# Attention with part of its exponentials on VectorE: one of three bit shifts becomes an accumulating DMA

## The chip, the core and the metric

The kernel runs on one core of a Trainium2 chip. The core has TensorE (PE), VectorE (DVE), ScalarE (ACT), GpSimd (POOL) and SyncE (SP), each with an instruction queue of its own that it works through in order, and 16 DMA engines that serve the queues of SP, ACT and POOL. The metric is the time of one execution on the device in microseconds (us), as a median of several runs. The profile shows one further execution, in which every instruction is recorded.

## The reference

Two attention blocks over the same 2048 tokens of width 512 with 32 heads of 16, mixed by a gate:

```python
def _A_ref(x, wqkv, wo):                       # B, S, D, H = 1, 2048, 512, 32
    q, k, v = ...                              # x @ wqkv, split into heads
    scores = jnp.einsum("bhqd,bhkd->bhqk", q, k) * (Dh ** -0.5)
    p = _softmax(scores, axis=-1)
    o = jnp.einsum("bhqk,bhkd->bhqd", p, v)
    return (...)(o) @ wo

def _B_ref(x, wqkv, w_phi, wo):                # linear attention
    phi_q = concat([softmax(q @ w_phi), softmax(-(q @ w_phi))])
    phi_k = ...                                # the same of k
    kv, z = ...                                # sums of phi_k * v and of phi_k over the tokens
    o = (phi_q @ kv) / (phi_q @ z + 1e-6)
    return (...)(o) @ wo

g = _sigmoid((x * gate_w).sum(-1, keepdims=True))
return g * a + (1 - g) * b
```

Nearly all the time goes to branch A: 32 heads x 2048 x 2048 scores, an exponential of each, and their product with the values. All inputs are bfloat16.

## The kernel before

Branch A is cut into 512 *packs*. A pack is one block of 128 keys (`kt`, 16 of them) for one chunk of 512 queries (`qc`, 4 of them) and 4 heads (`g8`, 8 groups): four score tiles of 128 keys x 512 queries. The 16 packs of one `(qc, g8)` are a *group*; there are 32. For each tile PE makes the scores into PSUM (`_scores`, L963, four tiles side by side in the array), an engine makes the exponentials, and PE adds exponentials times values into one accumulator bank (`_values`, L1077, again four tiles side by side). The denominators come from a column of ones among the values. `_norm` then transposes, divides and transposes back, on VectorE and, for all but the last groups, by way of 16 small `turned` copies and a DMA transpose on SP's queue.

The exponentials are made in two ways:

- By ACT, most of them: `_exp`, L1011, takes three tiles and two tiles in turn from a ring of five PSUM banks and writes `ET`. The score group after next (`_qk`) may start only when ACT has freed the banks.
- By VectorE, for the packs in `spot` (listed by `AWAY`, a bit mask for each group, at the places `KT0 + KTS * n`): `_vector_bits`, L903, multiplies the scores by a constant, adds another, and writes the result as unsigned 16-bit integers in `va`. Read as bfloat16 these bits are a straight-line approximation of the exponential. `_vector_terms`, L919, makes three copies of the bits shifted by 30, 62 and 95 in `vp`, for two packs at once. `_pv_terms` adds four products into the accumulator: `va` and the first copy with the values `V`, the second and third copy with `vc`, the values times 0.75 (`o_vc`). The sum of the four lines is a closer approximation.

Beside this, PE, VectorE and SP carry the projections of q, k and v (`_proj*`, with 8 small DMAs that place each query tile in `qT`, L677), the gate (`_gate`), and branch B (`_b_*`), spread over the whole span. PE also runs matmuls on zeros (`_fill`, L1084) and on unused data (`pads`, L984).

The order on every engine is not that of the program text. `Plan.order` sets up all operations with assumed lengths (`cost`), latencies (`lat`) and due times (`prio`), moves the due times by the hand-written-out list `SHIFT`, and lists the operations engine by engine: whatever can start first goes first, ties by due time. `Plan.emit` writes these five queues out, with semaphore waits where an operation needs another engine's. So any changed length moves operations everywhere, and in the chip an operation that is late holds up all that stands behind it in its engine's queue.

At the end, the last group's normalization (`_norm_last`) runs in two halves of 256 columns, and the last four output tiles (`_out`) are evicted by VectorE (two) and ACT (two).

## Time and profile before

| | |
|---|---|
| median of 3 runs | 759.11 us (758.89 to 759.82) |
| the profiled execution | 759.64 us, of which the span from the first to the last instruction is 757.8 us |
| mean granted TensorE clock | 0.999 of full speed |
| 20 us stretches from 40 to 740 us: ACT busy | 19.39 us or more in each |
| the same stretches: VectorE busy | 16.55 us (40 to 60), 18.51 to 20.00 in the others |
| DMA queue of SP: share of the 16 engines' span | 13.8%, 20.10 MB |
| last exponential ends | 748.63 us |

An engine's busy time is the time in which at least one of its instructions ran; consecutive instructions overlap a little, so that the mean of one is longer than its share of the busy time. "Idle before" is time in which the engine stood still just before an instruction of the group, and the name behind the arrow is what ended most of it. The timeline gives the start, the length, the engine, the line of the code and the shapes, with equal neighbours merged.

### The profile page before, as it was taken

How to read it: one execution, taken by the hardware profiler on the slowest of the kernel's cores; microseconds unless marked ns; L12 is line 12 of the kernel's file. 1: busy time of each engine (PE TensorE's matmuls, PEld its weight loads, DVE VectorE, ACT ScalarE, POOL GpSimd, SP SyncE). 2: the span in 40 equal slices, each digit the busy share in tenths (PEclk: the TensorE clock that was granted, in tenths of full speed). 3: DMA queues.
4: the chain of work that ended last, by engine and by line, in shares of the span. 5: the costliest groups of instructions: out<-in, count | busy, mean ns of one | idle time of the engine just before them, and what ended most of it. 6: DMA issues, size and time to landing. Idle time of an engine off the chain costs nothing.

```text
span 757.8 us, 16775 instructions
## 1 busy us (share of the span) xinstructions
PE 718.0 (95%) x7172; PEld 229.8 (30%) x7241; DVE 730.0 (96%) x1138; ACT 740.4 (98%) x646; POOL 8.1 (1%) x17
## 2 busy tenths in 40 slices
PE   8999999999999999999999999999999998999997
PEld 3334333342322232232222222223232222222222
DVE  6989899999999999999999999999999999999997
ACT  6999999999999999999999999999999999999995
POOL 3000000000000000000000000000000000000000
PEclk9999999999999999999999999999999999999999
DMA  9300100000010010000003101411103102301120
GB/s 212 130 2 1 15 8 10 14 7 16 2 16 8 8 16 8 6 11 7 18 9 63 23 12 25 71 29 23 29 29 65 21 16 35 78 13 25 12 26 29
DMA packets 88745, 21.68 MB, mean 29 GB/s; under 512 B 81632, under 2 KB 88160, under 8 KB 88672
## 3 DMA queue, kind: packets, MB, share of 16 engines
q1 hardware_dynamic: 86944, 20.10, 13.8%
q8 instruction: 56, 0.92, 0.5%
q10 hardware_dynamic: 1728, 0.52, 0.3%
q14 instruction: 17, 0.14, 0.1%
HBM read 4.21 MB, written 2.10 MB: 8 GB/s over the span
## 4 chain that ended last, share of the span: by engine, by line
ACT 64%; DVE 21%; PE 12%; DMA 1%; issue 1%; SPq 1%; DVEq 0%
ACT ET L1011 62%; DVE va L903 9%; DVE vp L919 6%; PE ps L963 5%; PE ps L1077 3%; ACT bq L1281 3%; PE ps L641 2%; DVE btree L1270 1%; DVE bq L1279 1%; PE ps L714 1%; DVE T L1129 1%; SPq L677 1%; DMA xT<-in_A_x_dram 1%; PE ps L984 1%; DVE V L720 1%
## 5 line engine op out<-in xcount | busy, mean ns | idle before, releaser
L1011 ACT ACTIVATE ET<-ps 128x1536 bf16<-128x1536 f32 x626 | 712.2, 1345 | 7.1 <-PE ps L963 6.2
L963 PE MATMUL ps<-qT,kT 32*128 32x512 bf16 x2048 | 312.1, 384 | 17.7 <-ACT ET L1011 8.5
L903 DVE TENSOR_SCALAR va<-ps 128x512 uint16<-128x512 f32 x484 | 314.4, 681 | 6.3 <-PE ps L963 4.9
L919 DVE TENSOR_SCALAR vp<-va 128x4096 uint16<-128x4096 uint16 (+1 forms) x204 | 221.6, 1097 | 0.2
L963 PEld LDWEIGHTS ps<-qT,kT 32*128 32x128 bf16 x2048 | 80.8, 91 | 263.0 <-ACT ET L1011 157.2
L1077 PE MATMUL ps<-ET,V 128*32 128x512 bf16 x1564 | 149.0, 386 | 0.3
L1077 PE MATMUL ps<-vp,vc 128*32 128x512 bf16 x968 | 84.5, 384 | 0.9 <-DVE vp L919 0.9
L1077 PEld LDWEIGHTS ps<-ET,V 128*32 128x32 bf16 x1564 | 39.3, 95 | 65.0 <-issue 51.0
L641 PE MATMUL ps<-WB,xT 128*128 128x512 bf16 x169 | 50.8, 383 | 4.4 <-issue 1.5
L1084 PE MATMUL ps<-kT,zero 128*32 128x512 bf16 x580 | 50.2, 385 | 0.0
L1077 PE MATMUL ps<-va,V 128*32 128x512 bf16 x484 | 47.8, 385 | 0.0
L1077 PE MATMUL ps<-vp,V 128*32 128x512 bf16 x484 | 46.2, 384 | 0.7 <-DVE vp L919 0.6
L641 PE MATMUL ps<-xT,WA 128*128 128x512 bf16 (+1 forms) x107 | 30.6, 373 | 3.6 <-issue 2.3
L1077 PEld LDWEIGHTS ps<-vp,vc 128*32 128x32 bf16 x968 | 21.9, 95 | 35.2 <-issue 18.0
L1281 ACT ACTIVATE bq<-bq 128x2048 bf16<-128x2048 bf16 x16 | 32.1, 2024 | 0.0
L1252 DVE CAST bq<-ps 128x512 bf16<-128x512 f32 x32 | 21.7, 683 | 2.9 <-PE ps L641 2.8
L1129 DVE STREAM_TRANSPOSE T<-ps 128x512 f32<-128x512 f32 x31 | 22.0, 709 | 0.6 <-PE ps L1077 0.3
L714 PE MATMUL ps<-WA,xT 128*128 128x128 bf16 x256 | 20.4, 220 | 0.5 <-DVE V L720 0.3
L1457 PE MATMUL ps<-WoA,onTA 128*128 128x512 bf16 x62 | 19.3, 382 | 1.0 <-DVE onTA L1117 0.9
L1279 DVE TENSOR_TENSOR bq<-bq,btree 128x2048 bf16<-128x2048 bf16 x16 | 19.4, 1214 | 0.0
L1084 PEld LDWEIGHTS ps<-kT,zero 128*32 128x32 bf16 x580 | 12.6, 94 | 22.1 <-issue 20.3
L641 PEld LDWEIGHTS ps<-WB,xT 128*128 128x128 bf16 x192 | 11.9, 97 | 23.9 <-issue 14.4
(87 smaller groups left out, 346.2 us busy)
## 6 DMA issues: line engine op xcount, KB each, us to landing
turned<-T SPq DMA_DIRECT2D x240, 8.0 KB, 1.8
qT<-qs SPq DMA_DIRECT2D x120, 16.0 KB, 1.8
WB<-in_B_wqkv_dram SPq DMA_DIRECT2D x1, 1536.0 KB, 7.4
out_dram<-WB SPq DMA_DIRECT2D x12, 128.0 KB, 1.9
WA<-in_A_wqkv_dram SPq DMA_DIRECT2D x3, 384.0 KB, 5.6
WoA<-in_A_wo_dram SPq DMA_DIRECT2D x1, 512.0 KB, 8.5
WoB<-in_B_wo_dram SPq DMA_DIRECT2D x1, 512.0 KB, 8.3
WA<-in_A_wqkv_dram ACTq DMA_DIRECT2D x3, 128.0 KB, 4.0
```

The lines of the kernel that those rows point to most:

```text
L641: ins = e.matmul(self._bank(job)[:, 0:n], lhs(c), rhs(c), start=(c == 0), stop=(c == 3))
L714: ins = e.matmul(self._bank(job)[:, P * tt:P * tt + P], self.xT[:, c, QCH * j + TOK * tt:QCH * j + TOK * tt + TOK], self.WA[:, 2, c, P * c ...
L903: parts.append(op("DVE", lambda e, j=j, job=job: e.tensor_scalar(self.va[:, pair, side, j, :], self._bank(job), SCALE * LOG2E * 128.0, (12 ...
L919: self.plan.op("DVE", lambda e, k=k, shift=shift: e.tensor_scalar(flat(self.vp[:, k]), flat(self.va[:, pair]), float(shift), None, op0=ALU ...
L963: return e.matmul(out, self.kT[32 * i:32 * i + 32, cp, kt * TOK:(kt + 1) * TOK], self.qT[32 * i:32 * i + 32, s, :], start=True, stop=True, ...
L1011: o = plan.op("ACT", lambda e: e.activation(self.ET[:, a % NS:a % NS + n, :], self.ps[:, self._ring(a):self._ring(a) + n, :], ACT.Exp, sca ...
L1077: ins = e.matmul(self._bank(ot)[32 * i:32 * i + 32, :], V[:, v0:v0 + 32], tile(), start=(kt == 0), stop=(kt == self.NT - 1), tile_position ...
L1084: ins = e.matmul(self._bank(ot)[32 * i:32 * i + 32, :], self.zero[:], self.kT[:, 0, 0:QCH], start=False, stop=False, tile_position=(0, 32 ...
L1129: op("DVE", lambda e: e.transpose(T1[:, side].rearrange("p b s -> p (b s)"), src()), 0.635, deps=last, writes=[b_T1[side]], name="n_t1", p ...
L1252: [lambda e, b, k=k: e.tensor_copy(bq[:, k].rearrange("p (g s v) -> p g s v", g=8, s=2)[:, :, 0, :], b.rearrange("p (g v) -> p g v", g=8))],
L1279: run("b_sub", two(2048), lambda e, out=out, t=t: e.tensor_tensor(out, p, spread(t[:, :, 0], 32), ALU.subtract), at, [pos, tree[side]], [buf])
L1281: op("ACT", lambda e, side=side: e.activation(sides[side], sides[side], ACT.Exp, scale=1.0 - 2 * side), self.c_act(2048) + 0.04, reads=[bu ...
```

## The change

- The first of the three shifts is no longer a copy. The first value product reads `va` as it is; then 30 is added to `va` in place; then the second value product reads `va` again. The two other shifts stay copies.
- The addition in place is a DMA on POOL's queue for 116 packs (`accum_op=ALU.add`, from `step`, a tensor in DRAM of 128 x 2048 numbers 30, written once at the start by a DMA from `va`, which POOL has filled), and an operation of VectorE for the ten packs in `IN_PLACE` (those of the last two groups). Each place of `va` has a semaphore of its own that counts its additions.
- `va` has three pairs of places in place of two, `vp` two shifts in place of three.
- The packs that VectorE works on stand at every second place (1, 3, 5, 7, 9 of a group) and no longer at every third, and are 126 in place of 121.
- The gate's sums are computed by narrow matmuls (32 columns of output rows, four chunks of queries side by side) into one bank, with one transpose, and spread by 16 small DMAs on SP's queue.
- The last group is normalized as the others before it, without halves; the order of the last output products changes.
- Assumed latencies of the query copies, `turned` copies and DMA transposes become longer, the due times and the whole list `SHIFT` are new, so that the order on every engine is another.

```diff
-SHIFTS = ((30, 0), (62, 1), (95, 1))
+SHIFTS = ((62, 1), (95, 1))
+FIRST_SHIFT = 30
...
-                if o.name.startswith("dma"):
+                if o.slot is not None:
+
+                    if o.slot not in places:
+                        places[o.slot] = ctx.enter_context(nc.semaphore(f"place{o.slot}"))
+                    count[o.slot] = count.get(o.slot, 0) + 16
+                    o.sem = (places[o.slot], count[o.slot])
+                elif o.name.startswith("dma"):
...
-    NB, LEAD = 4, 16.0
+    NB, LEAD, NVA = 4, 12.0, 3
+    VALUES, IN_PLACE, SLACK = 6.0, (480, 481, 482, 483, 484, 485, 486, 487, 488, 489, 490, 491, 492, 493, 494, 495, 496, 497, 498, 499, 500, 501, 502, 503, 504, 505, 506, 507, 508, 509, 510, 511), 6.0
...
-    KT0, KTS, NKT = 1, 3, 5
-    KEEP = 13
+    KT0, KTS, NKT = 1, 2, 5
+    KEEP = 14
...
-    TURN = 1.5
-    LAST, RAMP, PART = 8.0, 48, 24
-    STEP, BITS, TERM, PVX, NORM, QDUE, PUT = 0.625, -80, 5.5, 0.8, 2, -22.0, 3.8
+    TURN = 3.2
+    ADD, LANDING = 3.1, 2.6
+    LAST, RAMP, PART = 6.0, 48, 24
+    STEP, BITS, TERM, PVX, NORM, QDUE, PUT = 0.5, -40, -4, 0.8, 2, -22.0, 3.8
...
+        row = self.va[:, 0, 0].rearrange("p n q -> p (n q)")
+        o = op("POOL", lambda e: e.memset(row, FIRST_SHIFT), 2.0, prio=-60)
+        self.o_step = self.dma("SP", "step", lambda e: e.dma_start(self.step, row), cost=0.6, deps=[o], prio=-8, lat=4.0)
...
-                 prio=due, lat=1.6)
+                 prio=due, lat=2.8)
...
-            m = op("PE", mm, 4 * self.c_pe(512), reads=[self.b_xT[qc], b_gwb], name="gate", prio=self.GATE + qc, rel=self.GATE - 6,
-                   acquire=job)
...
+        def mm(e):
+            for c in range(4):
+                for qc in range(NQC):
+                    ins = e.matmul(self._bank(job)[32 * qc:32 * qc + 32, :], self.gwb[:, c, :],
+                                   self.xT[:, c, QCH * qc:QCH * qc + QCH], start=(c == 0), stop=(c == 3),
+                                   tile_position=(0, 32 * qc), skip_group_check=True)
+            return ins
...
+        parts = [lambda e, qc=qc, h=h: e.dma_start(self.gh[32 * h:32 * h + 32, :, qc, :], g[32 * qc:32 * qc + 32])
+                 for qc in range(NQC) for h in range(4)]
+        d = self.dma("SP", "gate", parts, cost=0.6 * len(parts), writes=[self.b_g], deps=[a], prio=self.GATE + 5, lat=1.6)
...
+        self.by_dma = self.spot - set(self.IN_PLACE)
...
+        pair, side = self.slots.pop(p)
+        va, b_va = self.va[:, pair, side], self.b_va[pair][side]
+        group = 16 * g
+
+        def values(tile, deps, reads, prio, tag, V=None):
+            src = {i: lambda i=i: tile()[:, i, :].bitcast(BF16) for i in range(4)}
+            x = self.plan.op("PE", lambda e: self._values(e, ot, g8, kt, src, V), 0.23, deps=deps, reads=reads, name="pvx",
+                             prio=prio, kind="col", array=0.2133)
+            x.tiles, x.tag = [0, 1, 2, 3], tag
+            self.late.append(x)
+            return x
+        ready = [self.pvs[self.NT * g]] + self.b_V[g8 // 2][kt // 4].writers
+
+        first = values(lambda: va, ready, [b_va], max(group + 1, p - self.VALUES), f"i{p}")
+        if p in self.by_dma:
+            add = self.dma("POOL", f"add{p}", lambda e: e.dma_start(va.rearrange("p n q -> p (n q)"), self.step, accum_op=ALU.add),
+                           cost=self.ADD, deps=b_va.readers + [self.o_step], prio=p - self.VALUES + 1, lat=self.LANDING)
+            add.slot = 2 * pair + side
+            add.fn = [add.fn]
+        else:
+            flat = va.rearrange("p n q -> p (n q)")
+            add = self.plan.op("DVE", lambda e: e.tensor_scalar(flat, flat, float(FIRST_SHIFT), None, op0=ALU.add),
+                               0.07 + self.NB * QCH * 0.00026, deps=list(b_va.readers), name="v_step", prio=p - self.VALUES + 1)
+        add.tag = f"i{p}"
+        b_va.readers = [values(lambda: va, ready + [add], [], p + self.PVX, f"x{p}")]
...
-        if g == self.NPACK // self.NT - 1:
-            return self._norm_last(qc, lambda: self._bank(self.ot[g]), last, self.onTA[:, qc % 2, g8 // 2, :], 16 * g + 17.0,
-                                   self.ot[g])
...
-                     lat=1.6)
+                     lat=2.6)
...
-                b_on = self.b_last[tt // 2] if final and pr == 3 else b_onTA[pr]
-                m = op("PE", mm, self.c_pe(512), reads=[b_on, self.b_WoA], deps=[m], name="outa",
-                       prio=due + (final and pr == 3), acquire=job if alone else None)
+                m = op("PE", mm, self.c_pe(512), reads=[b_onTA[pr], self.b_WoA], deps=[m], name="outa",
+                       prio=self.NPACK + 5 + (1, 0, 3, 2)[tt] if final and pr == 3 else due, acquire=job if alone else None)
```

In `_values` nothing changes; `_vector_terms` now hands `_pv_terms` the place of `va` (`self.slots`) and only the two remaining copies.

## The prediction

> **What bounds the kernel now.** I read the page's totals first, then the groups of instructions with shapes kept apart, then the table of waits, the DMA issues, and the timeline of the end.
>
> ```profile
> span 757.8 us, 16775 instructions
> PE 718.0 (95%) x7172; PEld 229.8 (30%) x7241; DVE 730.0 (96%) x1138; ACT 740.4 (98%) x646; POOL 8.1 (1%) x17
> ...
> L1011 ACT ACTIVATE ET<-ps 128x1536 bf16<-128x1536 f32 x626 | 712.2, 1345 | 7.1 <-PE ps L963 6.2
> L903 DVE TENSOR_SCALAR va<-ps 128x512 uint16<-128x512 f32 x484 | 314.4, 681 | 6.3 <-PE ps L963 4.9
> ```
>
> ScalarE (ACT) sets the time: 740.4 of 757.8 us busy, 712.2 of them exponentials. They cover 313 x 3 + 312 x 2 + 1 = 1564 score tiles, so a tile costs 712.2 / 1564 = 0.455 us, and an average exponential 712.2 / 626 = 1.14 us. Their idle is 7.1 us, of which 4.9 is one wait before the first. VectorE, at 96%, is nearly a second bound; POOL has nothing to do. So the time can fall only by taking tiles from ACT, and only if PE keeps it fed.
>
> ```profile
> PEld ps L963 <- ACT ET L1011: 157.2, 396, 1.0
> ...
> ACT ET L1011 <- PE ps L963: 6.2, 5, 4.9
> ```
>
> The first line is PE's cover: 396 times a score group stood ready and waited for ACT, 157.2 / 396 = 0.40 us each. A hold-up of PE's queue shorter than that costs nothing; what is longer reaches ACT. The second shows that it now hardly ever does.
>
> **The change, part by part.** The counts come from the two programs' order of instructions.
>
> *ACT.* 121 VectorE packs become 126: exponentials 313 + 312 + 1 become 309 + 308 + 1, that is 20 tiles fewer, 20 x 0.455 = -9.1 us on the path that sets the end. The gate's exponential shrinks from 128x128 to 128x32, -0.1 us.
>
> *VectorE.*
>
> ```profile
> L919 DVE TENSOR_SCALAR vp<-va 128x4096 uint16<-128x4096 uint16 x159 | 191.5, 1214 | 0.2
> ...
> L919 DVE TENSOR_SCALAR vp<-va 128x2048 uint16<-128x2048 uint16 x45 | 30.1, 682 | 0.0
> ```
>
> The bits grow from 484 to 504: +20 x 0.650 = +13.0. The shifts fall from 159 wide and 45 narrow to 116 and 20: 116 x 1.204 + 20 x 0.669 = 153.1 against 221.6, -68.5. Ten in-place adds of the narrow shape: +6.7. Three gate transposes fewer at 0.71: -2.1; the unsplit last norm -0.9. So 730 becomes 678 us, 91% of a span near 748. It is off the path, the gain is only room.
>
> *PE.* Values 3500 to 3560 matmuls, fillers 580 to 660, pads 56 to 34, gate 16 full ones to 16 narrow ones. At 0.095, 0.087 and 0.34 us of busy time each (149.0 / 1564, 50.2 / 580, 15.4 / 45): +5.7 + 7.0 - 7.5, and about -2.7 for the gate. The total stays within 3 us of 718; the 0.40 us waits hide it. Without them it would cost those 3 us.
>
> *SyncE.* Sixteen gate copies follow the first query load. Sixteen `turned` copies took 11.21 us to issue (74.16 in the timeline), so about 11 us; the queue was empty from 34 to 74 us, which hides them, and the first norm's `turned` waits behind them. The `step` store sits between WB (issued at 16.20) and WoA, which moves two weight loads that nobody needs before branch B's output by some 0.5 us. If that room were gone the first query load would be late instead, and it stands ahead of them.
>
> *The end.*
>
> ```profile
> 749.79 0.45 DVE L1107 STREAM_TRANSPOSE T<-ps 128x256 f32<-128x256 f32 x1 [0.55 <-PE ps L1077]
> ...
> 752.90 0.60 ACT L1468 ACTIVATE xT<-ps 128x512 bf16<-128x512 f32 x1 [4.27 <-PE ps L1457]
> ...
> 753.24 0.45 DVE L1117 STREAM_TRANSPOSE onTA<-T 128x256 bf16<-128x256 bf16 x1
> ...
> 754.38 0.60 ACT L1468 ACTIVATE xT<-ps 128x512 bf16<-128x512 f32 x1 [0.89 <-PE ps L1457]
> ```
>
> Now the last norm runs in two halves, from 749.79 to the last eviction's end at 754.98: 5.2 us. Unsplit: transpose 0.71, product 0.17, reciprocal 0.20, multiply 0.42, transpose 0.71, with gaps 2.3; first output matmul 0.39 and its delay 0.1; two evictions of 0.69 in a row on VectorE (ACT's two run beside them): 4.2 us. So -1.0.
>
> *The adds.* POOL issues 116 accumulating DMAs of 128x2048 uint16, 512 KB each, and PE waits for each before it reads `va` the second time. Behind that wait on PE stand the next score group and so the next exponential. Behind an add on POOL stands the next add only. No row of before has such a DMA. Nearest rows:
>
> ```profile
> WB<-in_B_wqkv_dram SPq DMA_DIRECT2D x1, 1536.0 KB, 7.4
> out_dram<-WB SPq DMA_DIRECT2D x12, 128.0 KB, 1.9
> WoA<-in_A_wo_dram SPq DMA_DIRECT2D x1, 512.0 KB, 8.5
> ```
>
> Between 128 KB (1.9 us) and 1536 KB (7.4 us) lie 3.9 us per 1000 KB, so 512 KB lands after 3.4 us if it is alone, and 1024 KB, since an add also reads its destination, after 5.4. WoA's 8.5 was queued with two other loads. The issue itself: 0.43 us is the single one of WB on SP's queue; the order in the diff assumes ADD = 3.1 on POOL and then LANDING = 2.6. Low end 0.43 + 3.4 = 3.8 us from release to landing, high end 3.1 + 5.4 = 8.5. I take the diff's sum, 5.7: it lies between the two, near their middle of 6.2, and the change calls its lengths recorded.
>
> What the order allows I counted as exponentials between the point where an add is released (first read on PE, and VectorE's shifts of that tile) and the PE group that needs it: 4 for five adds, 5 for three, 6 for 24, 7 for 16, 8 or more for 68. At 1.14 us that is 4.55, 5.7, 6.8, 8.0 and more. At 5.7 only the five are late, by 1.15 us, of which 0.40 is covered: 5 x 0.75 = +3.8 us. At 3.8 nothing is late. At 8.5, 48 are: 5 x 3.95 + 3 x 2.8 + 24 x 1.7 + 16 x 0.5 - 48 x 0.40 = +58 us. For the second of a pair POOL has two issues to do: 2 x 3.1 + 2.6 = 8.8, and those have 9 or more exponentials, 10.3 us.
>
> The Trainium skill (DMA: Bandwidth & Descriptors, "Anatomy of one DMA — SWDGE (gpsimd) path") fits a DMA issued from POOL at 2.0 us plus its bytes at 436 GB/s; an estimate from that page is 3.2 us for 512 KB and 4.4 for twice that, so by it no add is late and the sum is 3.8 us lower. The rows of before can't test it, as POOL issued nothing.
>
> *The sum.* 757.8 - 9.1 - 0.1 - 1.0 + 3.8 = 751.4 us of span. Around the span lay 759.64 - 757.8 = 1.8 us, and the profiled execution stood 0.5 above the median 759.11. So 751.4 + 1.8 - 0.5 = 752.7, rounded to 752.5.
>
> **The rivals.**
>
> *A, late adds hold PE (slower).* If release to landing is over the order's 5.7 us, each of the tight adds stops PE's queue with the score groups behind it. The gain of 10.2 us is eaten from 6.7 us on: 5 x (2.15 - 0.40) + 3 x (1.0 - 0.40) = 10.6. At 7.5: 5 x 2.95 + 3 x 1.8 + 24 x 0.7 - 32 x 0.40 = 24, so 747.6 + 24 + 1.3 = 773 us; at 8.0 it is +40 and 789. For it: the high end 8.5 is above 6.7, and the adds share the DMA engines with `turned` and query copies, which the diff now plans at 2.6 and 2.8 us where the trace has 1.8. Against it: the engines are 15% busy, and two thirds of the adds are far from tight.
>
> *B, POOL's issuing and VectorE's shifts get in each other's way.* The price: if a shift could not run while POOL issues, 116 x 3.1 = 360 us, 48% of the span, would be closed to 146 shifts and in-place adds, each waiting 1.55 us on average when it meets one: 146 x 0.48 x 1.55 = 109 us, VectorE 787, and with its idle 28 us 815. It decides from some 42 us on (748 - 678 - 28). With issues of 0.43 us it would cost 146 x 0.07 x 0.2 = 2 us and show nowhere. In before both engines work at once only in the first 21 us, too short to tell. The Trainium skill (SBUF — State Buffer, "SBUF: two separate sides") has such a rule: VectorE in a two-port mode and GpSimd take turns at a shared port pair, and descriptors issued from GpSimd wait meanwhile. By that rule the adds get longer too, by up to one shift, and A is likelier; no run here shows it yet.
>
> *C, no change.* PE, at 95% busy, takes back the 10 us in switches between scores and values of five more packs. Against it stands the 157.2 us of waiting for ACT. 758 to 760 us.
>
> **How the numbers follow.** 0.2% of 759, 1.5 us, is about what a measurement tells from no change. Forecast 0.50, with its own range 746 (nothing late, ACT's small gaps gone as well) to 757; A 0.36; B 0.07; C 0.07. Faster 0.50, all of it the forecast; slower 0.42, A and B less a hundredth that falls within; same 0.08. The range runs from 746 to 788, A up to a total of 8.0 us; left out are B, A's upper part and a little below.
>
> **What would show it.** Right: 618 exponentials at 1.14 us, ACT idle of some 12 us, VectorE near 91%, hardly any wait of the value matmuls on `va` for a DMA, and adds landing within 6 us of their release. Wrong: waits of PE for `va`'s DMA by the dozen with ACT's idle for scores grown by tens of us (A); shifts longer than 1.2 us or gaps before them, VectorE still at 96% or more (B); the exponentials fewer, but gaps before them ended by scores that waited for nothing but PE's own work (C). An eviction end more than 4.7 us after the last norm's start would make the end's term wrong.

## The result and the profile after

| | before | changed |
|---|---|---|
| median | 759.24 us (758.89 to 759.82) | 817.84 us (811.18 to 827.13) |
| the profiled execution's span | 757.8 us | 812.9 us |
| mean granted TensorE clock | 0.999 | 0.953 |

The ratio is 1.0742, with a 95% interval of 1.066 to 1.0824: the change makes the kernel 7% slower. 752.5 us was forecast. Of the four runs after, the one at 827.13 us was in a slower state; the other three have a median of 814.66, and from here on differences and the table below use such undisturbed runs alone.

The totals of the page after:

```profile
span 812.9 us, 17167 instructions
PE 747.4 (92%) x7359; PEld 228.6 (28%) x7359; DVE 692.6 (85%) x1092; ACT 738.2 (91%) x638; POOL 117.2 (14%) x134
```

ScalarE (ACT) is busy for 738.2 us and stands still for 812.9 - 738.2 = 74.7; before it was 757.8 - 740.4 = 17.4. So of the 55.1 us that the span grew, idle time of ACT gives +57.3 and its work -2.2. Idle time is the whole loss. The groups of the same page (busy us, mean ns; then the idle time before them and what ended most of it):

```profile
L1045 ACT ACTIVATE ET<-ps 128x1536 bf16<-128x1536 f32 x618 | 709.4, 1292 | 65.8 <-PE ps L997 64.2
L935 DVE TENSOR_SCALAR va<-ps 128x512 uint16<-128x512 f32 x504 | 329.1, 682 | 66.7 <-PE ps L997 64.6
...
L1112 POOL DMA_DIRECT2D va<-step x116 | 107.6, 1057 | 619.7 <-PE ps L1130 299.2
...
L1130 PE MATMUL ps<-va,V 128*32 128x512 bf16 x1008 | 96.2, 400 | 22.6 <-DMA va<-step 22.1
...
L1130 PEld LDWEIGHTS ps<-va,V 128*32 128x32 bf16 x1008 | 25.3, 96 | 67.2 <-DMA va<-step 36.0
```

The exponentials fell to 618 as meant, but ACT and VectorE both waited some 65 us for scores (`ps`, L997). PE had not made them, because it stood in its queue before the second product of `va` (L1130), 36.0 us before weight loads and 22.1 us before matmuls, all of it ended by an add that landed. The table of waits (us in total, times, longest) says how many these were:

```profile
ACT ET L1045 <- PE ps L997: 64.2, 48, 6.9
...
PEld ps L1130 <- DMA va<-step: 36.0, 43, 6.6
...
PE ps L1130 <- DMA va<-step: 22.1, 21, 6.3
...
PEld ps L997 <- DMA qT<-qs: 7.2, 4, 2.8
PE ps L1407 <- DMA phiT<-bq: 6.7, 1, 6.7
...
PE ps L997 <- DMA step<-va: 5.4, 1, 5.4
```

The rows of PEld and PE must not be added up: a weight load and the matmul behind it stand still in the same stretch of time, and all 21 waits of the matmuls end with a landing that one of the 43 weight loads waited for too. So 43 of the 116 adds held PE up, for 36.0 us in all, some by over 6 us. Waits for other transfers come on top, for query copies (`qT`, 7.2 us) and for a transpose of branch B (`phiT`, 6.7). The last line is a wait that the prediction doesn't have: at the start, the first scores for VectorE wait for the store of `step`. The DMA queues (packets, MB, share of the 16 engines' span) and the issues (KB each, median us to landing):

```profile
q0 software_dynamic: 16704, 60.82, 42.9%
...
va<-step POOLq DMA_DIRECT2D x116, 512.0 KB, 7.2
turned<-T SPq DMA_DIRECT2D x240, 8.0 KB, 4.0
```

An add lands 7.2 us after its issue at the median (5.3 at least, 13.9 at most). The prediction counts from the release on, that is from the end of the first product or of the shift, whichever is later. Read add by add from the trace, 51 adds were issued within 2 us of the one before; they landed 9.3 us after their release at the median, where 8.8 was taken, and the other 65 after 6.0, where 5.7 was taken. The slowest took 14.7. In engine time it costs 0.429 x 812.9 / 116 = 3.0 us of all 16 DMA engines. SyncE's `turned` copies, 1.8 us before, take 4.0. The chain that ended last shows both kinds of hold (start, length):

```profile
16.36 8.96 DMA step<-va
...
526.97 11.90 DMA va<-step
...
607.42 12.78 DMA va<-step
```

The store of `step` lies on the chain for 9 us at the start, and two adds for 12 us each further on. In stretches of 20 us (busy time and instructions of each engine, granted clock, share of the DMA engines, GB/s) these three places stand out:

```profile
20.00:40.00 20.00, 14.15 (x131) 4.20 (x132) 10.74 (x18) 12.95 (x12) 0.29 (x1) 0.83 0.38 126
...
520.00:540.00 20.00, 13.59 (x142) 3.93 (x139) 15.39 (x24) 14.44 (x13) 1.75 (x2) 0.87 1.11 158
600.00:620.00 20.00, 16.36 (x168) 4.69 (x166) 17.52 (x26) 17.99 (x16) 4.37 (x5) 1.00 1.02 137
```

ACT's figure is the one with x12, x13 and x16: 12.95, 14.44 and 17.99 us of 20. In the second and third stretch the DMA engines are full (1.11 and 1.02; a packet is counted whole in the stretch in which it starts, so a share can pass 1). The timelines of POOL and of SyncE's queue say with what:

```profile
526.97 1.75 POOL L1112 DMA_DIRECT2D va<-step  x2 [8.11 <-DVE vp L952]
```

```profile
522.04 6.28 SPq L1385 DMA_TRANSPOSE phiT<-bq  x4
531.37 10.96 SPq L1170 DMA_DIRECT2D turned<-T  x16
```

Two adds leave POOL within 1.75 us, since one wide shift of VectorE releases both; that alone is 6 us of all engines. Four transposes of SyncE stand before them, and 16 `turned` copies come behind.

Rival B had asked for longer shifts. They are unchanged, 1217 ns here and 1214 before:

```profile
L952 DVE TENSOR_SCALAR vp<-va 128x4096 uint16<-128x4096 uint16 x116 | 140.9, 1217 | 2.8 <-PE ps L1130 2.1
```

POOL's issues do get longer beside a shift. The longest stand here (the first line is two issues, of 1.71 and 3.03 us):

```profile
498.68 3.56 POOL L1112 DMA_DIRECT2D va<-step  x2 [20.97 <-PE ps L1130]
...
499.02 1.28 DVE L952 TENSOR_SCALAR vp<-va 128x4096 uint16<-128x4096 uint16 x1
...
500.95 1.21 DVE L952 TENSOR_SCALAR vp<-va 128x4096 uint16<-128x4096 uint16 x1
```

15 of the 116 issues overlap a shift in time and take 1.52 us at the median, up to 3.03; the other 101 take 0.86. So the issue waits for the shift and not the shift for the issue, and it happens rarely.

The end, from the last norm's start to the end of the last eviction:

```profile
805.77 0.72 DVE L1151 STREAM_TRANSPOSE T<-ps 128x512 f32<-128x512 f32 x1 [2.10 <-PE ps L1130]
...
808.89 1.09 ACT L1489 ACTIVATE xT<-ps 128x512 bf16<-128x512 f32 x2 [3.65 <-PE ps L1479]
```

808.89 + 1.09 - 805.77 = 4.2 us, as forecast.

### The profile page after: what moved, and what is told of

Its sections match the earlier page's. It is cut to its first block, busy times and chain, and to the rows that moved or that the text cites. A ratio compares the mean times of both kernels' runs of the same rounds, so it can differ in the third digit from the quotient of the medians.

```text
span 812.9 us, 17167 instructions
## 1 busy us (share of the span) xinstructions
PE 747.4 (92%) x7359; PEld 228.6 (28%) x7359; DVE 692.6 (85%) x1092; ACT 738.2 (91%) x638; POOL 117.2 (14%) x134
## 3 DMA queue, kind: packets, MB, share of 16 engines
q0 software_dynamic: 16704, 60.82, 42.9%
## 4 chain that ended last, share of the span: by engine, by line
PE 28%; ACT 25%; DVE 21%; DMA 18%; SPq 6%; issue 1%; POOL 0%; DVEq 0%
ACT ET L1045 23%; DMA va<-step 14%; PE ps L997 10%; PE ps L1130 9%; DVE va L935 8%; DVE vp L952 5%; PE ps L655 3%; SPq L1385 2%; DMA qT<-qs 2%; PE ps L1137 2%; SPq L691 2%; SPq L770 1%; ACT bq L1303 1%; PE ps L1433 1%; DMA step<-va 1%
## 5 line engine op out<-in xcount | busy, mean ns | idle before, releaser
L935 DVE TENSOR_SCALAR va<-ps 128x512 uint16<-128x512 f32 x504 | 329.1, 682 | 66.7 <-PE ps L997 64.6
L997 PE MATMUL ps<-qT,kT 32*128 32x512 bf16 x2048 | 312.6, 396 | 20.1 <-DMA qT<-qs 5.8
L1112 POOL DMA_DIRECT2D va<-step x116 | 107.6, 1057 | 619.7 <-PE ps L1130 299.2
L952 DVE TENSOR_SCALAR vp<-va 128x4096 uint16<-128x4096 uint16 (+1 forms) x136 | 154.1, 1139 | 3.2 <-PE ps L1130 2.4
L997 PEld LDWEIGHTS ps<-qT,kT 32*128 32x128 bf16 x2048 | 78.1, 91 | 273.5 <-ACT ET L1045 129.4
L1130 PE MATMUL ps<-ET,V 128*32 128x512 bf16 x1544 | 151.4, 396 | 1.0 <-DVE va L935 0.4
L1130 PE MATMUL ps<-va,V 128*32 128x512 bf16 x1008 | 96.2, 400 | 22.6 <-DMA va<-step 22.1
L1130 PE MATMUL ps<-vp,vc 128*32 128x512 bf16 x1008 | 88.4, 391 | 1.0 <-DVE vp L952 1.0
L1137 PE MATMUL ps<-kT,zero 128*32 128x512 bf16 x660 | 62.2, 414 | 0.0
L1130 PEld LDWEIGHTS ps<-ET,V 128*32 128x32 bf16 x1544 | 39.1, 95 | 67.5 <-issue 54.6
L655 PE MATMUL ps<-WB,xT 128*128 128x512 bf16 x192 | 56.7, 388 | 0.2
L1130 PEld LDWEIGHTS ps<-va,V 128*32 128x32 bf16 x1008 | 25.3, 96 | 67.2 <-DMA va<-step 36.0
L655 PE MATMUL ps<-xT,WA 128*128 128x512 bf16 (+1 forms) x128 | 37.1, 380 | 4.5 <-DVE va L935 4.0
L1130 PEld LDWEIGHTS ps<-vp,vc 128*32 128x32 bf16 x1008 | 24.0, 96 | 34.1 <-issue 17.5
```

The source lines that it names most:

```text
L655: ins = e.matmul(self._bank(job)[:, 0:n], lhs(c), rhs(c), start=(c == 0), stop=(c == 3))
L935: parts.append(op("DVE", lambda e, j=j, job=job: e.tensor_scalar(self.va[:, pair, side, j, :], self._bank(job), SCALE * LOG2E * 128.0, (12 ...
L952: self.plan.op("DVE", lambda e, k=k, shift=shift: e.tensor_scalar(flat(self.vp[:, k]), flat(self.va[:, pair]), float(shift), None, op0=ALU ...
L997: return e.matmul(out, self.kT[32 * i:32 * i + 32, cp, kt * TOK:(kt + 1) * TOK], self.qT[32 * i:32 * i + 32, s, :], start=True, stop=True, ...
L1112: add = self.dma("POOL", f"add{p}", lambda e: e.dma_start(va.rearrange("p n q -> p (n q)"), self.step, accum_op=ALU.add), cost=self.ADD, d ...
L1130: ins = e.matmul(self._bank(ot)[32 * i:32 * i + 32, :], V[:, v0:v0 + 32], tile(), start=(kt == 0), stop=(kt == self.NT - 1), tile_position ...
```

## The experiments

The first twelve keep the changed kernel's order on every engine, as its planner lists it, and edit what an operation does or what it waits for; e8 inserts operations into this order and e10 moves some. The last four list the order anew. Each ran beside the kernel before, at 759.6 to 760.4 us in these rounds. The table has them together; ratios are to the kernel before. For e4 the range of its four times stands in place of a median.

| | what | median, us | ratio (95%) |
|---|---|---|---|
| e1 | adds of 32 columns | 757.05 | 0.996 (0.9947 to 0.9974) |
| e2 | adds of half the columns | 764.94 | 1.0073 (1.0053 to 1.0094) |
| e3 | copies in place of adds | 766.35 | 1.0077 (1.0053 to 1.0101) |
| e4 | whole adds that PE doesn't wait for | 781.97 to 812.97 | none |
| e5 | as e1, and the scores don't wait for `step` | 747.88 | 0.9842 (0.9827 to 0.9857) |
| e6 | adds by POOL itself | 1136.93 | 1.4938 (1.4886 to 1.4989) |
| e7 | as e1, each add 6 us of POOL later | 1116.51 | 1.4698 (1.4674 to 1.4723) |
| e8 | 58 adds by VectorE, 58 by DMA | 785.87 | 1.0342 (1.0313 to 1.0372) |
| e9 | the change, scores don't wait for `step` | 803.0 | 1.0556 (1.0508 to 1.0604) |
| e10 | as e9, second product later on PE | 793.79 | 1.0491 (1.0415 to 1.0567) |
| e11 | as e1, each add 3 us of POOL later | 791.1 | 1.0393 (1.0323 to 1.0463) |
| e12 | as e9, branch B's transposes as copies | 792.56 | 1.0407 (1.0374 to 1.0439) |
| e13 | listed anew, half of the adds by VectorE | 767.98 | 1.01 (1.007 to 1.013) |
| e14 | listed anew, all adds by DMA | 838.13 | 1.1059 (1.0993 to 1.1125) |
| e15 | as e14, branch B's transposes as copies | 824.41 | 1.0844 (1.0798 to 1.0889) |
| e16 | as e14, copies in place of adds | 792.94 | 1.0437 (1.0383 to 1.0492) |

### e1, e2, e3: the size and the kind of the transfer

```diff
-e.dma_start(va.rearrange("p n q -> p (n q)"), self.step, accum_op=ALU.add)
+e.dma_start(va.rearrange("p n q -> p (n q)")[:, 0:32], self.step[:, 0:32], accum_op=ALU.add)    # e1
+e.dma_start(va.rearrange("p n q -> p (n q)")[:, 0:1024], self.step[:, 0:1024], accum_op=ALU.add)  # e2
+e.dma_start(va.rearrange("p n q -> p (n q)"), self.step)                                          # e3
```

> Each accumulating DMA adds only the first 32 of 2048 columns of va (64 bytes a partition); all waits and the order of every engine stay as in the changed kernel. Leaves out: the addition of 30 to the other columns. T1 (PE's queue waits for late adds): an add lands about 2 to 3 us after its release, inside the planned 5.7, no value matmul waits for it: 750 to 756 us. T2 (the adds' 61 MB slow SyncE's query, turned and transpose copies, which hold PE): there is no traffic left either, so also 750 to 756; it is told apart from T1 by the run without the wait. T3 (the new order itself is worse): 790 us or more.

> Half of each add: 1024 of 2048 columns, order and waits unchanged. Leaves out: the addition of 30 to the other half. The adds' packets took 42.9% of 16 engines in a span of 812.9 us, 3.0 us an add; half would be 1.5 us, and a landing 1.5 us earlier alone and some 2 us earlier in pairs, so 7.2 becomes 5.0 to 5.7, just about the planned 5.7. T1: 758 to 775 us, most of the loss gone with half the bytes. T2: proportional to bytes, about 785. T3: 810.

> The DMA copies the 30s over va in place of adding them, so it doesn't read its destination; order, waits, source and bytes written unchanged. Leaves out: the sum, the second product is of constants. If reading the destination is what makes an add long, the landing falls from 7.2 to 4 to 5 us and T1 expects 755 to 770 us; if the bytes written or the read from DRAM set it, the landing stays near 7 and the time near 815 us. T3: 810.

With 32 columns (116 issues and semaphores as before, 1.6% of the bytes) the time is 757.05 us, 57.6 less than the changed kernel's. No wait for `va` is left; what is left is one hold at the start:

```profile
ACT ET L1045 <- PE ps L997: 14.6, 8, 5.4
...
PE ps L997 <- DMA step<-va: 5.9, 1, 5.9
```

So POOL's issuing costs little, and the loss hangs on the transfers' bytes. Half of them cost 764.94 - 757.05 = 7.9 us, all of them 57.6: far from in proportion. An add of 256 KB lands 4.7 us after its issue, and none holds PE; of those of 512 KB, 43 do. The copy has the same 60.82 MB and the same packets, and its queue reads

```profile
q0 software_dynamic: 16704, 60.82, 23.8%
```

0.238 x 764.2 / 116 = 1.57 us of engine time, against 3.0 for the add, and it lands after 4.6 us. So at equal bytes the adding nearly doubles the transfer's engine time, and without it 814.66 - 766.35 = 48.3 us of the loss are gone. Whether the extra time goes into reading the destination or into the sum, these runs don't tell apart.

### e4: traffic without the wait

PE's second product reads `kT` in place of `va` and doesn't wait; only the next bits written to the place do.

```diff
-        b_va.readers = [values(lambda: va, ready + [add], [], p + self.PVX, f"x{p}")]
+        x = values(lambda: self.second(va, p), ready + [add], [], p + self.PVX, f"x{p}")
+        b_va.readers = [x]
...
+            x.deps.remove(add)
+            for o in self.plan.ops:
+                if x in o.deps and o.name in ("vqk", "v_bits"):
+                    o.deps.append(add)
```

> The adds run as in the changed kernel, with all their bytes, but PE does not wait for them: the second product reads kT in place of va; the next bits written to the same place wait for the add instead. Order unchanged. Leaves out: the second product of VectorE's packs (it is of other data). T1: 755 to 768 us (what is left are the waits for the step store, 5.4 us, and for SyncE's late copies). T2: 790 to 815 us, as the traffic is all there. T3: 790 or more.

I had expected the gain to come back whole. The profiled execution is the longest of the four, so its waits say which kinds there are, not what they cost on average:

```profile
ACT ET L1058 <- PE ps L1010: 64.9, 39, 9.3
...
PE ps L1010 <- DMA qT<-qs: 15.8, 5, 8.3
...
PE ps L1010 <- DMA step<-va: 6.6, 1, 6.6
PE ps L1422 <- DMA phiT<-bq: 6.4, 1, 6.4
PE ps L1010 <- DMA va<-step: 5.9, 2, 4.7
```

With no product of `va` waiting, PE is held by SyncE's transfers instead: the query copies, which the next chunk's scores need, and a transpose of branch B. So the adds cost by their traffic too, 25 us (781.97 - 757.05) even in the best of the four. This part was not in my sum at all.

### e5, e9: the store of `step`

The step's numbers are stored from the last place of `va` in place of the first, and only the first bits written there wait for the store. e5 has adds of 32 columns, e9 whole ones.

```diff
-        row = self.va[:, 0, 0].rearrange("p n q -> p (n q)")
+        row = self.va[:, 2, 1].rearrange("p n q -> p (n q)")
...
+            if self.o_step in o.deps and o.slot is None:
+                o.deps.remove(self.o_step)
+        for o in self.guard:
+            o.deps.append(self.o_step)
```

> The run with adds of 32 columns, and besides the 30s are stored to DRAM from the last of the six places of va, so that the first bits and the score matmul before them no longer wait for the step store; order unchanged. Leaves out: the addition of 30 to the other columns. In the 32-column run PE waited 5.9 us for the store and ACT's idle before exponentials was 14.6 us, 5.4 of it at once. Expected under every theory: 757.1 less 5 to 6, 751 to 752 us, which is what the new order is worth without late adds and without their traffic. If the wait is only replaced by the next one, 756 to 757.

> The changed kernel with the whole adds and waits; only the 30s are stored from the last of the six places of va, so that the first bits do not wait for the store. Order unchanged. The whole computation is done. Expected: the changed kernel's 817.8 less the 5.4 us wait and up to the 9.2 us that the same edit saved with adds of 32 columns: 806 to 814 us.

```profile
span 746.5 us, 17095 instructions
PE 709.3 (95%) x7286; PEld 228.9 (31%) x7359; DVE 689.8 (92%) x1092; ACT 730.6 (98%) x638; POOL 118.2 (16%) x134
```

e5 is the change's order with nothing late: 747.88 us, and ACT 98% busy. My sum without the adds' term is 757.8 - 9.1 - 0.1 - 1.0 = 747.6 of span; e5 has 746.5. Against e1, the store alone costs 9.2 us, though PE's wait for it is 5.9: in the stretch from 20 to 40 us PE's granted clock is also lower, 0.66 in e1 and 1.00 in e5. In the whole change it is 814.66 - 803.0 = 11.7 us. e9 keeps the computation of the reference, and 803.0 - 747.88 = 55.1 us remain for the adds.

### e6: the adds on POOL itself

```diff
+            add.fn = lambda e, flat=flat: e.tensor_scalar(flat, flat, float(FIRST_SHIFT), None, op0=ALU.add)
```

> Each add of the 116 is done by POOL's own ALU (tensor_scalar, 128x2048 uint16, in place) in place of a DMA; no store of 30s; every other instruction and the order unchanged. The whole computation is done. POOL's memset of the same shape took 1.81 us. If an add takes 1.8 to 4 us it ends before the planned 5.7: 750 to 754 us, and both T1 (late adds) and T2 (traffic) expect that. If POOL and VectorE's shifts exclude each other (rival B), shifts grow from 1.22 us or POOL's adds far beyond 2 us, and the time is 760 to 800 us.

```profile
L436 POOL TENSOR_SCALAR va<-va 128x2048 uint16<-128x2048 uint16 x116 | 647.9, 5585 | 413.0 <-PE ps L1145 282.6 <-DVE vp L966 124.9 <-DVE ghb L790 1.2
L966 DVE TENSOR_SCALAR vp<-va 128x4096 uint16<-128x4096 uint16 x116 | 286.5, 2472 | 2.5 <-PE ps L1145 1.9
```

VectorE's wide shift, 1217 ns in the change, takes 2472 here. So POOL's and VectorE's *operations* do hold each other up, which is rival B's mechanism. POOL's *issuing of DMAs* leaves the shifts at 1217 and is itself the one that waits. The add takes 5.6 us of POOL, and the time grows by half, far above both expected ranges.

### e7, e11: lateness without traffic

Adds of 32 columns, and before each POOL clears a small scratch tile several times: 14 times in e7 (374 ns each on average), 6 times in e11 (407 ns).

```diff
+                for _ in range(6):
+                    if done[0]:
+                        e.wait_ge(sem, done[0])
+                    e.memset(self.idle[:], 0).then_inc(sem, 1)
+                    done[0] += 1
```

> Lateness without traffic: adds of 32 columns, but POOL clears a scratch of 256 columns fourteen times before each, some 4 to 5 us, so that an add lands about 7 us after its release as in the changed kernel, without the bytes. Order unchanged. Leaves out: the addition of 30 to the other columns. T1 (PE's queue waits for late adds): 775 to 800 us, with waits of the value matmuls for va of 20 us and more. T2 (the traffic is what costs): 757 to 765 us.

> Lateness without traffic, milder than before: adds of 32 columns, POOL clears the scratch six times before each (a clearing took 0.37 us), so POOL is taken 2.2 + 0.9 us for each add, as long as the DMA engines were for a whole one (3.0 us), and the first of two adds lands some 4.9 us after its release, the second some 8 us, which is inside or at the planned 5.7 and 8.8. Leaves out: the addition of 30 to the other columns. T1: 757 to 775 us, against 757.1 with no lateness and 1116.5 with 6 us of POOL for each. If the time is far above, the order has no room at all for a queue on POOL.

e7 made the adds far later than they are in the change: they land 14.2 us after their release at the median, the second of a pair later still, since POOL does both one after the other. Its time, 1116.51, far above the range expected, shows only how steep the price gets: 359 us over e1. e11 is nearer, some 3.3 us of POOL for each add, like the 3.0 us of the DMA engines in the change, and nothing but that is late:

```profile
PEld ps L1140 <- DMA va<-step: 31.0, 42, 3.4
...
PE ps L1140 <- DMA va<-step: 16.4, 19, 3.1
```

42 adds held PE, for 31.0 us in all, beside 43 and 36.0 us in the change. The time is 791.1 us, 34 over e1, without any traffic. Six clearings and the issue take POOL 2.6 to 5.7 us, and the small add lands 2.4 us after its issue, nearly the lengths that the diff's order assumes, 3.1 and 2.6. By the count of the prediction some five to eight adds should have been late by them; 42 held PE.

e5 shows why, because nothing is late there. The time from an add's release to the start of its second product on PE, its room, is 5.7 us at least, 7.7 at the median and 11.9 at most in e5's trace. The planned order itself has 5.7, 7.6 and 11.9. The 65 adds that the change issued alone or first have 6.2 at the median, the 51 others 9.3: only some 0.5 us over the 5.7 and 8.8 that the list assumes. In e11 the adds land 4.4 to 12.6 us after their release, 7.0 at the median, and 40 of them later than their room in e5.

### e8: half of the adds on VectorE

The 58 adds with the least room become operations of VectorE, put into its queue at their planned time; the other 58 stay DMAs; the store as in e9.

```diff
+            add.fn = lambda e, flat=flat: e.tensor_scalar(flat, flat, float(FIRST_SHIFT), None, op0=ALU.add)
+            q = self.plan.queues["DVE"]
+            q.insert(next(i for i, o in enumerate(q) if o.start >= add.start), add)
```

> The 58 adds with the least time in the order go to VectorE (0.68 us each, 39 us in all, of its 62 us of idle), put into its queue at their planned time; the other 58 stay DMAs; the 30s are stored from the last place of va. The whole computation is done. Half the traffic, and the remaining adds have 7.5 us or more: T1 expects hardly a wait for them; T2 expects what half the bytes cost, some 5 us as in the run with half adds. Either: 754 to 762 us. If VectorE's inserted adds delay its evictions by more than its idle covers: 765 or more.

785.87 us, 17 better than e9, and above the 754 to 762 expected. Only two waits for an add are left, of 1.1 us in all, but each inserted 0.68 us delays the bits and shifts behind it. PE's matmuls of scores wait for those instead (1.7 us in all in e9):

```profile
PE ps L1017 <- DVE va L953: 14.7, 42, 1.1
```

### e10: more room before the second product

As e9, with the second product moved back in PE's queue by up to 5 us of planned time, as far as its own users allow; the median room of an add grows from 8 to 11 exponentials.

```diff
+                q.insert(j, q.pop(i))
```

> As the run with the store moved, and besides every value matmul that needs an add stands up to 5 us later in PE's own queue (not past the work that waits for it); all other queues unchanged. The exponentials between release and need rise from a median of 8 to 11 (9.1 to 12.5 us). The whole computation is done and all the traffic is there. T1 (PE waits for late adds): the waits for va fall from 58 us of matmuls and weight loads to under 15, and the time to 765 to 785 us. T2 (traffic through SyncE's late copies): 795 to 812 us.

793.79 us; the profiled execution was 27 us longer than that, so its waits tell kinds and not sums. The intervals of e10 and e9 overlap: three exponentials more of room, 3.4 us, gained nothing that is clear of the noise. Fewer adds held PE (16 in place of 38), but longer (up to 9.3 us). A landing that is always 7.2 us would have been covered in most places, so something makes some adds much later than that; the slowest here took 18.1 us from its issue.

### e12: the collision with SyncE's transposes

As e9, with the 32 DMA transposes of branch B made plain copies of the same tiles.

```diff
-        return self.dma("SP", name, lambda e: e.dma_start_transpose(out, src), ...
+        return self.dma("SP", name, lambda e: e.dma_start(out, src.rearrange("p (t q) -> p t q", q=P)) if name[:2] in ("ph", "nb") else e.dma_start_transpose(out, src), ...
```

> The kernel of e9 (all adds whole, the store of the step moved; 803.0 us) with the 32 DMA transposes of branch B (phiT and WT) replaced by plain copies of the same tiles, so that these tiles are not transposed and branch B's part of the output is not the reference's. The engines' order is the same. Theory 'collision with the transposes': the longest holds of PE by an add's landing stand in the stretches 440 to 460, 520 to 540 and 600 to 620 us, in which the phiT transposes are under way and the 16 DMA engines are nearly full; without transposes the share of engine time of SP's queue falls from 14.9 % to below 11 %, phiT lands in under 3 us, the wait of 6.8 us for phiT is gone, the longest landing of an add falls from 13.1 to below 10 us and the time from 803 to 775 to 788 us. Rival 'the adds themselves': pairs of adds issued 0.86 us apart need 6 us of all engines, so the long landings come with or without transposes; then the time stays within 795 to 805 us, and the waits of PE for va's DMA stay near 45 us.

792.56 us, 10.4 less than e9. The two stretches in which PE stood still in the change are filled (ACT 12.16 and 16.14 us of 20 in e9):

```profile
520.00:540.00 20.00, 18.64 (x213) 5.37 (x213) 18.23 (x28) 19.64 (x18) 3.66 (x5) 1.00 0.83 143
...
600.00:620.00 20.00, 19.73 (x204) 5.63 (x201) 18.91 (x29) 19.68 (x18) 3.48 (x4) 1.00 0.85 160
```

and the longest waits shrink (5.8 us in e9), while the many short ones stay (38 adds held PE in e9, for 28.9 us):

```profile
PEld ps L1140 <- DMA va<-step: 32.4, 49, 2.5
...
PE ps L1140 <- DMA va<-step: 16.8, 22, 2.2
PE ps L1417 <- DMA phiT<-bq: 6.1, 1, 6.1
```

Both theories are partly right. The holds of 5 to 6 us are gone with the transposes; but 44.7 us over e5 (792.56 - 747.88) are left with plain copies in their place, an add still takes up to 12.8 us to land, and the wait for `phiT` stays.

### e13 to e16: is it the order or the adds?

The planner lists the order anew, with a new `SHIFT` and with an add's lengths nearer to what was measured. e13 does the first add of most pairs on VectorE, so that 62 DMAs are left (58 were expected); e14 keeps all 116.

```diff
-    ADD, LANDING = 3.1, 2.6
+    ADD, LANDING = 0.9, 6.0   # e13
+    ADD, LANDING = 3.1, 6.0   # e14
-    SHIFT = (...)
+    SHIFT = (...)
```

> The whole computation, listed anew by the kernel's own planner with a new SHIFT, an add's landing assumed at 6.0 us after an issue of 0.9 (6.9 in place of 5.7), the first add of each pair an operation of VectorE and the second a DMA (58 DMAs), the step stored from the last place of va. Planned end 754.7 us; the kernel before had 751.5 planned and 757.8 us of span, the changed order 740.0 planned and 746.5 in e5, so 6.4 us come on top and 1.4 outside the span. Theory 'the list was at fault': 762 to 766 us, hardly a wait of PE for va's DMA, ACT idle under 30 us. Rival 'the traffic holds SyncE's copies and PE anyway': 770 to 785 us, with waits for qT, phiT and va by the dozen. Either way it should be faster than e8 (785.87), which had the same split in a frozen order, and slower than the kernel before.

> As e13_half, with all 116 adds as DMAs, 3.1 us of POOL and 6.0 us of landing assumed for each (9.1 us for one, 12.2 for the second of a pair). Planned end 767.8 us, so 775.5 if nothing is late. Theory 'the list was at fault': 773 to 780 us, few waits for va, turned copies late (4 us) but nobody waiting for them. Rival 'the traffic': 785 to 805 us, near e9's 803.0, with waits for qT, phiT or va of over 20 us in all.

e14 came out the longest of its kind, 838.13 us, above the ranges of both theories and in spite of its room. Its profiled execution is 852.07 us, at a lower clock than the other three; its waits are read for where they stand:

```profile
PE ps L1303 <- DMA phiT<-bq: 24.7, 1, 24.7
PEld ps L893 <- DMA qT<-qs: 11.2, 5, 3.7
...
PE ps L893 <- DMA qT<-qs: 9.7, 5, 3.4
```

No wait of PE for `va` is among them: the longer lengths did give the adds enough room. In its place stand waits for SyncE's transfers, one of 24.7 us:

```profile
440.00:460.00 20.00, 16.97 (x202) 4.79 (x194) 17.78 (x26) 18.58 (x17) 5.76 (x6) 1.00 1.13 127
460.00:480.00 20.00, 0.00 (x0) 0.00 (x0) 0.00 (x0) 0.00 (x0) 0.00 (x0) 0.50 1.08 87
```

In the second stretch no engine does anything; only the DMA engines are full. Six adds left POOL from 442.7 to 456.7 us and four `phiT` transposes left SyncE from 446.8 on, and the last of these landed after 28 us. At 3.0 us for each, six adds are 18 us of all engines.

e13, with about half of the traffic, is the best version with adds by DMA that computes the reference: 767.98 us, no wait for `va` above 0.6 us, `phiT` landing within 6.7. That is just above the 762 to 766 of the first theory. It is still 1% slower than the kernel before, and 18 us faster than e8, which has about the same split in the change's order.

e15 and e16 edit e14 as e12 and e3 edited the change:

> e14_all with the 32 DMA transposes of branch B as plain copies of the same tiles (these tiles aren't transposed, so branch B's part of the output is another). Theory 'transposes and adds that meet stall each other': phiT lands in under 10 us at most, the hold of 24.7 us is gone, the longest landing of an add falls from 26 to under 14, time 800 to 818 us (842 less some 25 to 40). Rival 'six adds within 14 us are enough': phiT still lands after over 20 us in that place, time 830 to 845 us.

> e14_all with each add a plain copy of the same 512 KB (nothing is added; the second product reads 30 in each place). Theory 'the reading and adding makes the load': engines at 1.6 us for each in place of 3.0, phiT lands in under 8 us, nothing waits for long, time 773 to 780 us, the 775.5 of its plan. Rival 'any 512 KB beside the transposes does it': over 800 us with phiT landing after more than 15 us.

Both times lie between the ranges of the two theories. Without transposes 13.7 us are gone (838.13 - 824.41), and `phiT` lands after 14.2 us at most. With copies of the same bytes 45.2 are gone (838.13 - 792.94), the queue's share is 22.0% in place of 41.2%, and hardly a DMA is waited for; what ACT still idles there lies mostly in this order, which is worse than the one of the diff. Put beside each other: taking the adding away, at equal bytes, is worth 48.3 us in the diff's order and 45.2 in the other. Between these two orders it changes *who* waits, PE's second product or SyncE's copies; the adds cost nearly the same in both.

## Why the prediction was wrong

**The right parts.** ScalarE bounds, and the new order is worth what the sum gave it: e5, with nothing late, has 746.5 us of span where the terms without the adds made 747.6. ACT's work fell by 740.4 - 730.6 = 9.8 us there (9.2 forecast). The gate copies on SyncE and the fillers on PE cost nothing that shows (PE 709.3 busy in e5, under the forecast 718), and the end took 4.2 us as worked out. VectorE's busy time came to 689.8 in e5 and not 678. The lengths of its instructions add up to 52.4 us less than before, as forecast, but with gaps between them fewer overlap; at 92% it has no consequence.

**The step that failed: the term for the adds, +3.8 us.** It measured 803.0 - 747.88 = 55.1 us. Three things went into it.

1. *The length.* "I take the diff's sum, 5.7" was near the middle: 6.0 us from release to landing for an add alone or first, and 9.3 in place of 8.8 for one issued behind another. But the choice leant on the diff's own constant, which is no measurement, and one figure stood for all adds. The slowest took 14.7 us. Two adds that leave together share the engines; meeting SyncE's transposes cost more (e12, 10.4 us; e15, 13.7), but the longest landing stayed at 12.8 us from the issue without them (e12).
2. *The room.* "What the order allows I counted as exponentials" made the room too large. In e5, 54 of the 116 adds have less than 7.2 us; the count had 32. At 7.2 us for each the prediction's own formula gives 5 x 2.65 + 3 x 1.5 + 24 x 0.4 - 32 x 0.40 = 14.6 us; with the rooms of e5, and 0.40 off for each late add, it gives 33. Against their own rooms in e5, 49 adds of the change landed too late: 22 of the 65 issued alone or first, and 27 of the 51 behind another, which the prediction had none of ("9 or more exponentials, 10.3 us"; in e5 they have 7.5 to 11.9). e11 shows the price without traffic, 34 us. The room is as large in the chip as in the list; the list just leaves half a microsecond beyond the lengths that it assumes. How much of the rest comes from one late add delaying the next bits in its place, and with them the next add, these runs don't tell.
3. *The engines.* "The engines are 15% busy" was said of the kernel before, as a reason against late adds. The adds themselves fill 42.9%, because each takes 3.0 us of all 16 where a copy of the same bytes takes 1.57. With that the `turned` copies went from 1.8 to 4.0 us, and PE waits for query copies and transposes too. In e4, where no product waits for an add, 25 us and more are lost all the same. No term of the sum had it.

**A second step that failed: the store of `step`.** "Moves two weight loads that nobody needs ... by some 0.5 us" looked at SyncE's queue only. The store reads the place of `va` that the first bits are written to, so these wait until it has landed (9.0 us), and PE's queue with them. That is 9.2 us in e5 against e1, and 11.7 in e9 against the change. It could have been foreseen: the wait stands in the changed program (`self.b_va[0][0].readers = [self.o_step]`).

**The rivals.** A is what happened, with the sign and the place that were given; its price, 773 us at 7.5 us of lateness, was far too low for the reasons 2 and 3. B has its mechanism but not its price: the shifts kept 1217 ns, an issue took 0.86 us at the median, and only 15 issues met a shift, for up to 3.03 us. C is false, since e5 is faster by 1.6%.

**The estimate and the rule that were cited.** The Trainium skill (DMA: Bandwidth & Descriptors, "Anatomy of one DMA — SWDGE (gpsimd) path") gave an estimate of 3.2 us for 512 KB. e1's adds of 8 KB landed after 2.6 us, near the 2.0 at which that fit begins; at 512 KB a plain copy took 4.6 and an add 7.2, so beside this kernel's other work, and for adding transfers above all, the measurement decides against it. The Trainium skill (SBUF — State Buffer, "SBUF: two separate sides") has VectorE and GpSimd take turns at a shared port pair. For operations e6 agrees with it (2472 ns for a shift in place of 1217). For descriptors issued from POOL the traces agree too: an issue that overlaps a shift takes 1.52 us in place of 0.86 in the change, and 0.95 in place of 0.53 in e3 (medians; 15 and 11 issues of 116).

## What to carry to other kernels

Here a transfer that adds into its destination cost about twice the engine time of a copy of the same bytes, and SyncE's small copies landed after 4.0 us beside it and after 2.3 beside the copies; before anything is moved to such a DMA, the sum of engine time it brings has its own line in the forecast. An order that is planned with assumed lengths can leave almost no room beyond them: read the room in microseconds from the plan or from a run in which nothing is late, not in counts of other work, measure one such operation at its real size, and set its slowest landings, not its middle, against that room. Waits of a weight load and of the matmul behind it are one wait, not two. And a one-time store at the start is looked at from its source buffer too: who has to wait before that may be written again?

## What the runs showed that was not expected

- An accumulating DMA of 512 KB costs 3.0 us of all 16 DMA engines (42.9% of 812.9 us for 116), a copy of as many bytes in as many packets 1.57 (e3). One of 8 KB takes POOL as long to issue as one of 512 KB: POOL 118.2 us busy in e1, 117.2 in the change. The copy's issue is shorter, 75.5 us of POOL in all.
- Where six such adds and four DMA transposes met, no compute engine did anything for 20 us, with the DMA engines full at 87 GB/s (the one execution of e14 that was profiled).
- An operation on POOL of 128x2048 16-bit integers takes 5.6 us and doubles VectorE's shifts to 2.47 us (e6), while POOL's issuing of 116 DMAs leaves them at 1217 ns and waits itself: a copy's issue takes 0.53 us alone and up to 1.56 beside a shift (e3).
- Where PE stood still, the granted clock was lower: 0.999 over the span before, 0.953 in the change, 0.773 in e6; e5, with PE busy throughout, has 1.000. In e14's 20 us without work it was 0.50.
